# A planned mLSTM and MoE kernel: wider first tiles, GpSimd as a second home for weight pieces, and a plan that reckons with TensorE's clock

## The chip, the cores and the metric

The kernel runs on one core of one Trainium2 chip. The core's engines are TensorE (PE in the profile; PEld is its weight loading), VectorE (DVE), ScalarE (ACT), GpSimd (POOL) and SyncE (SP), which issues the DMAs. Each works through its own queue in order, and semaphores tie the queues together. The metric is device microseconds (us) of one execution.

## The reference, cut to what matters

Four sequences of 768 steps with 8 heads of width 40 go through an mLSTM (a gated linear attention), and its 3072 x 320 result through two feed-forward blocks (called MoE here) of width 2048. All of it is float32.

```python
for t in range(S):                       # per batch and head
    m_new = max(f[t] + m, i[t])
    C = exp(f[t] + m - m_new) * C + exp(i[t] - m_new) * outer(v[t], k[t])
    n = exp(f[t] + m - m_new) * n + exp(i[t] - m_new) * k[t]
    y[t] = sigmoid(o[t]) * (C @ q[t]) / max(abs(n @ q[t]), 1.0)
x = y                                    # 3072 x 320
h = x @ w_in;  x = max(0.01 * h, h) @ w_out
h = max(x @ w_in2, 0);  out = (h * h) @ w_out2
```

## The kernel before, in words

The sequence is cut into 6 chunks of 128 steps. A chunk holds 4 batches, so it makes a block of 512 tokens. `attention(c)` does the mLSTM of a chunk in parallel form, in 8 groups of 4 heads (two groups a batch). On TensorE a group is a decay row spread over 128 partitions (L615, chunk 0 only), the scores (L635), the state's part (L645) and the values (L651, or L656 to L661 in bfloat16 thirds). Between them stand an exp on ScalarE (L626), a mask on GpSimd (L629) and a product on VectorE (L638). The two groups of a batch end in `hs` (L682 or L684), then in a denominator `d` (L736 to L738), the gated `y` (L740, L743), three transposes (L750) and the split of x into a high part `xH` (L755) and a low part `xL` (L756).

The MoE computes float32 products out of float32r ones, by high and low parts. `weight(layer, j)` loads one of 16 slices of a layer's weights, puts the high part into `w` (L401) and the low parts beside it: L405 (512 and 64 columns) and the "stack" L410 (64 x 128), all on VectorE. `moe_h` multiplies x by a slice (8 matmuls, L434) into `hp`, of which there are 2 buffers. ScalarE and VectorE make `gH` and `gL` of it (L440 to L442), and `out1` adds 8 matmuls (L465 to L467, L470, L471) into three accumulators. One slice on one block is 16 matmuls of up to 512 columns. Layer 0 and then layer 1 run over the 6 blocks, with the attention of later chunks in between.

Block 0 of layer 0 is done in two halves of 256 columns, since batches 0 and 1 are ready before 2 and 3. The second half runs `lag` = 7 slices behind the first (L765 to L772).

No engine's order is written by hand. `op(...)` records a node with an engine, an estimated duration and its buffers. `Sched.forward` (L137) plays these nodes with the estimates, `backward` (L113) turns the result into latest start times, and after six passes the best plan is issued. The keys of the first pass come from the table `ORDER`. When TensorE has nothing ready in the plan, a `warm` product may be put in: an empty matmul that only keeps TensorE at work, into `hp` (L322) or, adding zero, into an accumulator (L478). A node with `alt` may go to GpSimd instead of VectorE.

Of the kernel before, what the change touches and what calls it, by code (L numbers as in the profile page):

```python
# [30 lines left out]
ORDER = dict(pe0=7000, ld2=80, kv=-2.33, ks=6.4, g2=32.54, z=-15.1, lag=7, m0=0.71, o0=1.85, a04=-6.78, a0s=4.65, a1=29.4, a1s=5.72, a1ld=23.83, w0=-33.49, ws=2.64, bias=1.13, c0=-19.03, cs=13.0, cld=31.54, wl=1.51, outk=2.04)  # L31
SHARE = 0.6
PASSES = 6
# [13 lines left out]
class Node:  # L47
    __slots__ = ("eng", "dur", "fn", "key", "deps", "outs", "ndep", "ready", "allocs", "bufs", "end", "start", "table", "lat", "seq", "alt", "after", "first", "bank")


class Sched:
# [10 lines left out]
    def op(self, eng, dur, key, fn, r=(), w=(), table=None, lat=0, alt=None, after=0):  # L62
# [4 lines left out]
        n.eng, n.dur, n.fn, n.key, n.table, n.lat = eng, dur, fn, key, table, lat  # L67
# [69 lines left out]
    def forward(self):  # L137
# [24 lines left out]
        out, now, dma_free, done, last = [], 0.0, 0.0, 0, 0.0  # L162
        while done < len(self.nodes):

            for e, cand in ready.items():
# [3 lines left out]
                for n in sorted(cand, key=lambda n: (n.key, n.seq)):  # L169
                    if all(b.live or (b.first is n and queue[b.tag][-1] is b and free[b.tag] > 0) for b in n.bufs):  # L170
                        pick = n
                        break
                if pick is None:
                    if e == "PE" and self.idle and (now < 12000 or now - last > 300) and (fill := next((f for f in self.idle if f[1].live and f[2].start is None), None)):
                        n = Node()
                        n.eng, n.dur, n.fn, n.allocs, n.seq, n.start, n.key = e, 430 if now < 6800 else 215, fill[0], [], -1, now, 0
                        n.bufs, n.deps = [], []
                        out.append(n)
                        busy[e] = n
                        heapq.heappush(at, (now + n.dur, 0, -1))  # L180
                    continue
# [38 lines left out]
            if seq < 0:  # L220
                busy["PE"] = None
                last = now - 200
                continue
            n = self.nodes[seq]
            if what == 0:
                busy[n.eng] = None
                last = now if n.eng == "PE" else last
# [35 lines left out]
def mlstm_moe_kernel(  # L263
# [111 lines left out]
    def weight(layer, j, key):  # L375
# [49 lines left out]
    def moe_h(layer, c, lo, n, j, key, xk):  # L425
# [10 lines left out]
        op("PE", 8 * mm(n), key, pe, r=[(w, "H"), (w, "L"), (w, "C")] + [(x, k) for k in xk for x in (xH, xL)], w=[(hp, 0)])  # L436
# [14 lines left out]
    def out1(c, lo, n, j, key):  # L451
# [20 lines left out]

        rd = [(w, "H"), (w, "L"), (w, "Lc"), (gH, 0), (gL, 0)]
        op("PE", 3 * mm(n), key, lambda: ab(0, 256, 1024), r=rd, w=[(a[0], lo)])
        op("PE", 3 * mm(n), key, lambda: ab(1, 384, 1152), r=rd, w=[(a[1], lo)])
        x = op("PE", 2 * mm(n), key, cc, r=rd + ([(warm, 0)] if c == 0 and j == NF - 1 and lo == 0 else []), w=[(a[2], lo)])
        if j == NF - 1 and n < BLK and lo == 0:
            sc.idle.append((lambda: T.matmul(a[2].t, warm.t, zeros(), start=False, stop=False), a[2], x))  # L478
        if last:
            x2[c] = x = sb(f"x2_{c}", [128, 3, BLK])  # L480
            key -= 100
            rd = [[(a[t], l) for l in range(0, BLK, n)] for t in range(3)]
# [18 lines left out]
    def out2(c, j, key):  # L501
# [5 lines left out]
        for b in range(B):  # L507
# [9 lines left out]
            op("PE", 3 * mm(DM), key, pe, r=[(w, "H"), (w, "L"), (gH, 0), (gL, 0)], w=[(a, 0)])  # L517
# [11 lines left out]
    def attention(c, keys, ld):  # L529
# [23 lines left out]
        op("PE", 380, k0, gate_T, r=[(G_sb, f"A{p}"), (G_sb, f"c{p}"), (G_sb, f"w{p}"), (ident, 0)], w=[(gp, 0)])  # L553
# [305 lines left out]
```

## Time and profile before

| | |
|---|---|
| time, median of 3 runs | 857.66 us (857.45 to 859.22) |
| the profiled execution's own time | 857.15 us |
| its span, first to last instruction | 855.1 us |
| mean granted clock of TensorE | 0.988 |
| busy: TensorE, VectorE, ScalarE, GpSimd | 842.0, 541.4, 464.9, 77.8 us |

A row of a timeline gives the start, the time taken, the engine with the source line, the operands, and in brackets how long the engine was idle before and what ended that. Consecutive matmuls overlap in the records, so the time from start to start is what one costs. A matmul of float32 operands stands as two records. The clock is a share of full speed: 1.00 is 2.4 GHz and 0.50 is 1.2 GHz.

### The profile page before, as it was taken

The page shows a single profiled execution, that of the slowest core. Times are in us where ns is not written, and L with a number is a line of the kernel's source. Part 1 is how long each engine was busy: PE and PEld are TensorE (multiplying, and loading weights), DVE is VectorE, ACT ScalarE, POOL GpSimd, SP SyncE. Part 2 cuts the span into 40 slices and gives each one's busy share as a digit, 9 for nine tenths or more (in the row PEclk, how much of TensorE's full clock was granted, in tenths as well). Part 3 has the DMA queues.
Part 4 walks back from the last instruction along what each step waited for, and adds up shares of the span by engine and source line. Part 5 has one row for each costly group of instructions (what it writes and reads, how often), then busy time and mean ns, then how long its engine had stood idle before and what let it go on. Part 6 is the DMA issues. An engine that isn't in the chain of part 4 may idle for free.

```text
span 855.1 us, 14028 instructions
## 1 busy us (share of the span) xinstructions
PE 842.0 (98%) x5310; PEld 729.9 (85%) x5310; DVE 541.4 (63%) x1008; ACT 464.9 (54%) x946; POOL 77.8 (9%) x101
## 2 busy tenths in 40 slices
PE   9899999999999999999999999999999999999998
PEld 7689999788778788788888889999999999999997
DVE  7799876767676776667576899453443443533433
ACT  6577638656765776577455675343333433433332
POOL 2231204103010311011000000000000000000000
PEclk8899999999999999999999999999999999999999
DMA  8675325435343543453232442000000000000000
GB/s 226 222 233 183 118 73 181 140 111 172 103 137 114 165 138 109 152 166 118 77 103 72 165 136 69 1 31 1 1 32 1 14 17 1 31 1 1 32 1 31
DMA packets 52211, 78.60 MB, mean 92 GB/s; under 512 B 4336, under 2 KB 40784, under 8 KB 52144
## 3 DMA queue, kind: packets, MB, share of 16 engines
q1 hardware_dynamic: 52144, 77.71, 28.8%
q8 instruction: 42, 0.69, 0.3%
q14 instruction: 25, 0.20, 0.1%
HBM read 54.26 MB, written 4.01 MB: 68 GB/s over the span
## 4 chain that ended last, share of the span: by engine, by line
PE 82%; DVE 6%; ACT 4%; SPq 3%; DMA 3%; issue 1%; ACTq 0%; DVEq 0%
PE hp L434 36%; PE acc L465 4%; PE acc L467 4%; PE acc L466 4%; SPq L581 3%; PE acc L515 3%; PE acc L514 3%; PE acc L513 3%; PE attS L635 3%; PE acc L470 2%; PE atty L645 2%; PE acc L471 2%; PE atty L651 2%; DMA T<-X 2%; PE atty L515 1%
## 5 line engine op out<-in xcount | busy, mean ns | idle before, releaser
L434 PE MATMUL hp<-xH,w 128*128 128x512 f32 (+1 forms) x1040 | 294.8, 381 | 0.3 <-DVE gL L442 0.3
L434 PEld LDWEIGHTS hp<-xH,w 128*128 128x128 f32 x1040 | 183.5, 189 | 29.2 <-DVE gL L442 0.9
L434 PE MATMUL hp<-xL,w 128*128 128x512 f32 (+1 forms) x624 | 199.1, 375 | 0.0
L446 DVE TENSOR_TENSOR g<-g 128x512 f32<-128x512 f32 x96 | 66.3, 691 | 118.4 <-ACT g L445 118.3
L434 PEld LDWEIGHTS hp<-xL,w 128*128 128x128 f32 x624 | 115.9, 189 | 22.4
L445 ACT ACTIVATE g<-hp 128x512 f32<-128x512 f32 x96 | 57.3, 597 | 129.4 <-PE hp L434 129.4
L448 DVE TENSOR_TENSOR gL<-g,gH 128x512 fp32r<-128x512 f32 x96 | 66.4, 692 | 56.4 <-ACT gH L447 56.4
L447 ACT CAST gH<-g 128x512 fp32r<-128x512 f32 x96 | 59.6, 620 | 70.4 <-DVE g L446 70.4
L442 DVE TENSOR_TENSOR gL<-hp,gH 128x512 fp32r<-128x512 f32 (+1 forms) x112 | 68.3, 610 | 34.7 <-ACT hp L441 34.2
L465 PE MATMUL acc<-gH,w 128*128 128x512 f32 (+1 forms) x224 | 86.1, 384 | 0.0
L440 ACT ACTIVATE gH<-hp 128x512 fp32r<-128x512 f32 (+1 forms) x112 | 59.6, 532 | 48.4 <-PE hp L434 39.3
L467 PE MATMUL acc<-gL,w 128*128 128x512 f32 (+1 forms) x224 | 81.3, 363 | 0.0
L466 PE MATMUL acc<-gH,w 128*128 128x512 f32 (+1 forms) x224 | 81.0, 362 | 0.0
L515 PE MATMUL acc<-w,gL 128*128 128x320 f32 x192 | 59.3, 309 | 0.0
L514 PE MATMUL acc<-w,gH 128*128 128x320 f32 x192 | 59.3, 309 | 0.0
L513 PE MATMUL acc<-w,gH 128*128 128x320 f32 x192 | 59.2, 308 | 0.0
L441 ACT ACTIVATE hp<-hp 128x512 f32<-128x512 f32 (+1 forms) x112 | 59.1, 528 | 0.0
L626 ACT ACTIVATE aw<-aw,cs 128x128 f32<-128x128 f32 x160 | 50.8, 391 | 12.2 <-DMA aw<-Adram 12.1
L629 POOL TENSOR_SCALAR_AFFINE_SELECT aw<-aw 128x512 f32<-128x512 f32 x48 | 33.5, 697 | 196.5 <-ACT aw L626 174.0
L467 PEld LDWEIGHTS acc<-gL,w 128*128 128x128 f32 x224 | 42.6, 190 | 6.9 <-DVE gL L442 0.2
L465 PEld LDWEIGHTS acc<-gH,w 128*128 128x128 f32 x224 | 42.7, 191 | 5.3
L466 PEld LDWEIGHTS acc<-gH,w 128*128 128x128 f32 x224 | 42.8, 191 | 4.9
(163 smaller groups left out, 1515.1 us busy)
## 6 DMA issues: line engine op xcount, KB each, us to landing
T<-X SPq DMA_DIRECT2D x144, 120.0 KB
x<-in_wts_dram SPq DMA_DIRECT2D x16, 704.0 KB
aw<-Adram SPq DMA_DIRECT2D x40, 256.0 KB
nat<-in_nat_dram SPq DMA_DIRECT2D x24, 328.0 KB
qkr<-in_qk_dram SPq DMA_DIRECT2D x16, 360.0 KB
X<-in_wts_dram SPq DMA_DIRECT2D x8, 704.0 KB
T<-in_wts_dram SPq DMA_DIRECT2D x8, 704.0 KB
og<-in_og_dram SPq DMA_DIRECT2D x12, 320.0 KB
```

The source lines that it names most:

```text
L434: T.matmul(hp.t[:, 0:n], w.t[:, col:col + 128], x.t[:, kt, o], start=(s == 0), stop=(s == 7))
L440: op("ACT", act(n, True), key, lambda: A.activation(gH.t[:, 0:n], h(), AF.Prelu, alpha=0.01), r=[(hp, 0)], w=[(gH, 0)])
L442: op("DVE", dve(n), key, lambda: V.tensor_tensor(out=gL.t[:, 0:n], in0=h(), in1=gH.t[:, 0:n].bitcast(F32), op=ALU.subtract), r=[(hp, 0), ( ...
L446: op("DVE", dve(n), key, lambda: V.tensor_tensor(out=g.t, in0=g.t, in1=g.t, op=ALU.mult), r=[(g, 0)], w=[(g, 0)])
L447: op("ACT", act(n), key, lambda: A.copy(gH.t, g.t), r=[(g, 0)], w=[(gH, 0)])
L448: op("DVE", dve(n), key, lambda: V.tensor_tensor(out=gL.t, in0=g.t, in1=gH.t.bitcast(F32), op=ALU.subtract), r=[(g, 0), (gH, 0)], w=[(gL, 0)])
L465: T.matmul(a[t].t[:, o], w.t[:, hc:hc + 128], gH.t[:, 0:n], start=first, stop=False)
L466: T.matmul(a[t].t[:, o], w.t[:, lc:lc + 128], gH.t[:, 0:n], start=False, stop=False)
L467: T.matmul(a[t].t[:, o], w.t[:, hc:hc + 128], gL.t[:, 0:n], start=False, stop=last)
L513: T.matmul(a.t[:, 0:DM], gH.t[:, s], wH, start=first, stop=False)
L514: T.matmul(a.t[:, 0:DM], gH.t[:, s], wL, start=False, stop=False)
L515: T.matmul(a.t[:, 0:DM], gL.t[:, s], wH, start=False, stop=last)
```

## The change

- Block 0 in wider tiles: slices 0 to 6 are still done in halves. From slice 7 on (L797 to L804 of the changed kernel) one tile of 512 columns serves both halves, and the second half of slices 0 to 6 runs between these tiles. Nine slices go from 2 x 256 to 512 columns.
- The stack (L441, before L410) and low parts of at most 512 columns (L436, before L405) get `alt`, so the plan may give them to GpSimd. In the built program 14 of the 16 stacks, all 16 pieces of 64 columns and one of 512 columns of layer 0 are there, and 2 stacks of layer 1.
- The plan now models TensorE's clock: each TensorE node has a `load`, and where the plan finds too little of it, later nodes take twice their duration. An empty product is put in only where nothing is ready and the recent load is low. The old rule asked for an early time, or for 300 ns without work. Short attention pieces are marked `small`, are kept together, and a change to a long piece costs 85 ns in the plan.
- `ORDER` has new numbers. The plan before has 18 empty products into `hp` and 15 of L478, the changed one 15 and none.

```diff
-ORDER = dict(pe0=7000, ld2=80, kv=-2.33, ks=6.4, g2=32.54, z=-15.1, lag=7, m0=0.71, ...
+ORDER = dict(pe0=6853.31, ld2=74.38, kv=1.55, ks=6.4, g2=29.83, z=-14.43, lag=7, m0=0.89, ...
+WINDOW = 3413
+BUSY = 0.38
+KEEP = 0.43
+STAY = 3000
...
+        def clock():
+            return 1 if stream.get(int(now // WINDOW) - 1, 0) >= BUSY * WINDOW else 2
...
+        def idles():
+            while hist and hist[0][1] < now - WINDOW:
+                hist.pop(0)
+            return sum(r * (e - max(b, now - WINDOW)) for b, e, r in hist) < KEEP * WINDOW
...
-                        pick = n
-                        break
+                        if pick is None:
+                            pick = n
+                        elif n.small:
+                            pick = n
+                        if e != "PE" or pick.small or not small or n.key > pick.key + STAY:
+                            break
+                if e == "PE" and pick is None and idles() and (fill := next((f for f in self.idle if f[1].live and f[2].start is None), None)):
...
-                    if e == "PE" and self.idle and (now < 12000 or now - last > 300) and (fill := ...
...
+                if e == "PE":
+                    dur += 85 if small and not n.small else 0
+                    small = n.small
+                    dur *= clock()
+                    streams(n.load, dur)
...
-        op("DVE", dve(128), key, lambda: stack(V), r=[(fb, fr), (w, "C")], w=[(w, "C")])
+        op("DVE", dve(128), key, lambda: stack(V), r=[(fb, fr), (w, "C")], w=[(w, "C")], alt=("POOL", pool(128), lambda: stack(G)))
...
-            op("DVE", dve(n), key, lambda: low(V, o, n, s0), r=[(fb, fr), (w, "H")], w=w_)
+            op("DVE", dve(n), key, lambda: low(V, o, n, s0), r=[(fb, fr), (w, "H")], w=w_, **(dict(alt=("POOL", pool(n), lambda: low(G, o, n, s0))) if n <= 512 else {}))
...
-    LAG = ORDER["lag"]
-    for i in range(NF + LAG):
-        for s in range(2):
-            j = i - LAG * s
-            if 0 <= j < NF:
+    LAG = min(ORDER["lag"], NF // 2 - 1)
+    for i in range(max(NF, 2 * LAG)):
+        for s, j in ((0, i), (1, i - LAG)):
+            n = 256 if j < LAG else BLK
+            if 0 <= j < (LAG if s else NF):
                 key = ORDER["m0"] * U * i + s
-                moe_h(0, 0, 256 * s, 256, j, key, (2 * s, 2 * s + 1))
-                out1(0, 256 * s, 256, j, key + ORDER["o0"] * U)
+                moe_h(0, 0, 256 * s, n, j, key, (2 * s, 2 * s + 1) if n < BLK else range(4))
+                out1(0, 256 * s, n, j, key + ORDER["o0"] * U)
```

TensorE ahead of the first MoE matmul, before: L478 with `warm` is an empty product, L750 the transposes of `y`, L615 a decay row, L434 the first MoE matmul.

```order
L478 LDWEIGHTS warm
L478 MATMUL acc_239<-warm 128x512
L478 LDWEIGHTS warm
L478 MATMUL acc_239<-warm 128x512
L750 MATMUL attm<-ident,y 128x128 x3
L478 LDWEIGHTS warm
L478 MATMUL acc_239<-warm 128x512
L478 LDWEIGHTS warm
L478 MATMUL acc_239<-warm 128x512
L615 MATMUL attS<-G_sb,ident 128x128 x4
L434 MATMUL hp<-xH,w_334 128x256 x4
L434 MATMUL hp<-xL,w_334 128x256 x2
```

The same place in the changed order (L683 are the values of batch 1, L782 the transposes, L647 decay rows, L740 the update, L667 scores, L492 the zeroing of an accumulator, L465 the first MoE matmul):

```order
L683 MATMUL atty<-nat,aw 128x42 x4
L782 MATMUL attm<-ident,y 128x128 x3
L647 MATMUL attS<-G_sb,ident 128x128 x4
L740 MATMUL attm<-wv,nat 40x42 x16
L667 MATMUL attS<-w_132 128x128 x4
L782 MATMUL attm<-ident,y 128x128 x3
L492 LDWEIGHTS warm
L492 MATMUL acc_390<-warm 128x512
L647 MATMUL attS<-G_sb,ident 128x128 x4
L465 MATMUL hp<-xH,w_360 128x256 x4
L465 MATMUL hp<-xL,w_360 128x256 x2
```

The empty products are gone, and a score piece and its decay row have moved ahead of the second transposes.

GpSimd before, from the fifth mask on: L629 masks, L740 the gating of `y`, L696 a product with the gates.

```order
L629 AFFINE_SELECT aw<-aw 128x512 x2
L740 TENSOR_TENSOR og<-og,d 128x320
L629 AFFINE_SELECT aw<-aw 128x512
L696 TENSOR_TENSOR wv<-nat,ex 128x336 x2
L629 AFFINE_SELECT aw<-aw 128x512
L740 TENSOR_TENSOR og<-og,d 128x320
L629 AFFINE_SELECT aw<-aw 128x512 x3
```

The same place in the changed order (L661 masks, L772 the gating, L728 the product; L441 stacks and L436 low parts of weight slices, `w_360` being slice 0 and `w_476` slice 3):

```order
L661 AFFINE_SELECT aw<-aw 128x512 x2
L772 TENSOR_TENSOR og<-og,d 128x320
L661 AFFINE_SELECT aw<-aw 128x512
L441 TENSOR_TENSOR w_360<-x_2_270,w_360 64x128
L436 TENSOR_TENSOR w_360<-x_2_270,w_360 128x64
L441 TENSOR_TENSOR w_400<-x_3_362,w_400 64x128
L436 TENSOR_TENSOR w_400<-x_3_362,w_400 128x64
L728 TENSOR_TENSOR wv<-nat,ex 128x336
L661 AFFINE_SELECT aw<-aw 128x512
L728 TENSOR_TENSOR wv<-nat,ex 128x336
L441 TENSOR_TENSOR w_462<-x_2_270,w_462 64x128
L436 TENSOR_TENSOR w_462<-x_2_270,w_462 128x64
```

Between the same masks and products now stand two pieces of each weight slice. The mask behind `w_400` has four of them ahead of it.

TensorE at slice 7 of block 0, before (`w_779` is slice 7 and `w_334` slice 0): a half tile of slice 7, then the second half of slice 0.

```order
L434 MATMUL hp<-xH,w_779 128x256 x4
L434 MATMUL hp<-xL,w_779 128x256 x2
L434 MATMUL hp<-xH,w_779 128x256
L434 MATMUL hp<-xL,w_779 128x256
L434 MATMUL hp<-xH,w_334 128x256 x4
L434 MATMUL hp<-xL,w_334 128x256 x2
L434 MATMUL hp<-xH,w_334 128x256
L434 MATMUL hp<-xL,w_334 128x256
```

The same place in the changed order (`w_757` is slice 7, `w_360` slice 0): slice 7 with 512 columns, then the second half of slice 0.

```order
L465 MATMUL hp<-xH,w_757 128x512 x4
L465 MATMUL hp<-xL,w_757 128x512 x2
L465 MATMUL hp<-xH,w_757 128x512
L465 MATMUL hp<-xL,w_757 128x512
L465 MATMUL hp<-xH,w_360 128x256 x4
L465 MATMUL hp<-xL,w_360 128x256 x2
L465 MATMUL hp<-xH,w_360 128x256
L465 MATMUL hp<-xL,w_360 128x256
```

The half tile of slice 7 has become one of full width; the second half of slice 0 still follows it with 256 columns.

## Rows read from the trace of the kernel before

**Rows 1.** The page, engines: busy us, share, instructions.

```profile
PE 842.0 (98%) x5310; PEld 729.9 (85%) x5310; DVE 541.4 (63%) x1008; ACT 464.9 (54%) x946; POOL 77.8 (9%) x101
```

**Rows 2.** Busy time by stretch: length, PE, PEld, DVE, ACT, POOL, clock, DMA share, GB/s.

```profile
16.00:29.00 13.00, 13.00 (x54) 10.52 (x53) 8.92 (x20) 7.06 (x20) 1.53 (x2) 0.50 0.84 245
36.00:57.00 21.00, 20.62 (x183) 18.34 (x183) 20.51 (x40) 17.79 (x50) 7.46 (x7) 1.00 0.59 190
57.00:60.00 3.00, 3.00 (x16) 3.00 (x16) 3.00 (x7) 2.58 (x7) 2.07 (x3) 0.51 0.94 333
84.00:87.00 3.00, 3.00 (x17) 2.95 (x16) 2.56 (x5) 1.28 (x4) 1.15 (x2) 0.56 0.29 65
120.00:360.00 240.00, 234.09 (x1721) 195.55 (x1720) 170.31 (x349) 160.63 (x356) 42.99 (x55) 1.00 0.44 136
```

**Rows 3.** TensorE's waits by releaser: us in total, times, longest.

```profile
PE atty L645 <- DVE hs L686: 2.7, 4, 0.8
PE atty L659 <- DVE x L665: 1.9, 3, 1.3
```

**Rows 4.** Timeline of TensorE, 25 to 63 us: start, us, instruction, idle before.

```profile
25.53 1.93 PE L651 MATMUL atty<-nat,aw 128*128 128x42 f32 x8
35.39 0.72 PE L434 MATMUL hp<-xH,w 128*128 128x256 f32 x4
51.02 0.81 PE L478 MATMUL acc<-warm 128*128 128x512 bf16 x3
61.89 0.38 PE L478 MATMUL acc<-warm 128*128 128x512 bf16 x1
62.57 0.74 PE L434 MATMUL hp<-xH,w 128*128 128x256 f32 x4 [0.30 <-DVE gL L442]
```

**Rows 5.** Timeline of VectorE, 20 to 36 us.

```profile
20.13 0.68 DVE L638 TENSOR_TENSOR aw<-aw,acc 128x512 f32<-128x512 f32 x1
27.83 0.17 DVE L736 SCALAR_TENSOR_TENSOR d<-hs 128x8 f32<-128x8 f32 x1 [3.67 <-ACT hs L682]
30.99 1.21 DVE L405 TENSOR_TENSOR w<-x,w 128x512 fp32r<-128x512 f32 x1
34.34 0.55 DVE L756 TENSOR_TENSOR xL<-attm,xH 128x384 fp32r<-128x384 f32 x1
34.81 0.68 DVE L405 TENSOR_TENSOR w<-x,w 128x512 fp32r<-128x512 f32 x1
```

**Rows 6.** Timeline of TensorE, 57 to 69 us and 499 to 503 us.

```profile
57.30 0.41 PE L465 MATMUL acc<-gH,w 128*128 128x256 f32 x1
59.00 1.05 PE L434 MATMUL hp<-xH,w 128*128 128x256 f32 x4
66.64 0.74 PE L434 MATMUL hp<-xH,w 128*128 128x256 f32 x4
67.70 0.64 PE L434 MATMUL hp<-xH,w 128*128 128x256 f32 x4
68.65 0.28 PE L465 MATMUL acc<-gH,w 128*128 128x256 f32 x1
...
499.04 1.07 PE L434 MATMUL hp<-xH,w 128*128 128x512 f32 x4
502.67 1.07 PE L434 MATMUL hp<-xH,w 128*128 128x512 f32 x4
```

**Rows 7.** VectorE's groups by form, L410 and L405: count, busy us, mean ns, idle.

```profile
L410 DVE TENSOR_TENSOR w<-x,w 64x128 fp32r<-64x128 f32 x16 | 5.1, 317 | 0.5
L405 DVE TENSOR_TENSOR w<-x,w 128x64 fp32r<-128x64 f32 x16 | 4.5, 288 | 0.1
```

**Rows 8.** Timeline of GpSimd, 0 to 32 us.

```profile
1.07 0.29 POOL masks.py:199 TENSOR_SCALAR_AFFINE_SELECT ident<-ident 128x128 f32<-128x128 f32 x1
30.34 1.31 POOL L740 TENSOR_TENSOR og<-og,d 128x320 f32<-128x320 f32 x1 [7.58 <-PE attm L708]
```

More of the change, by code (lines that the diff above doesn't have):

```diff
@@ L47 @@
 class Node:
-    __slots__ = ("eng", "dur", "fn", "key", "deps", "outs", "ndep", "ready", "allocs", "bufs", "end", "start", "table", "lat", "seq", "alt", "after", "first", "bank")
+    __slots__ = ("eng", "dur", "fn", "key", "deps", "outs", "ndep", "ready", "allocs", "bufs", "end", "start", "table", "lat", "seq", "alt", "after", "first", "bank", "small", "load")
 class Sched:
@@ L161, in forward, with streams @@
                 heapq.heappush(at, (n.after, 1, n.seq))
-        out, now, dma_free, done, last = [], 0.0, 0.0, 0, 0.0
+        out, now, dma_free, done, small = [], 0.0, 0.0, 0, False
+        stream, hist = {}, []
+        def clock():
+            return 1 if stream.get(int(now // WINDOW) - 1, 0) >= BUSY * WINDOW else 2
+        def streams(load, dur):
+            t, r = now, load / dur
+            while t < now + dur:
+                k = int(t // WINDOW)
+                u = min(now + dur, (k + 1) * WINDOW)
+                stream[k] = stream.get(k, 0) + r * (u - t)
+                t = max(u, t + 1e-3)
+            hist.append((now, now + dur, r))
+        def idles():
+            while hist and hist[0][1] < now - WINDOW:
+                hist.pop(0)
+            return sum(r * (e - max(b, now - WINDOW)) for b, e, r in hist) < KEEP * WINDOW
         while done < len(self.nodes):
@@ L170, in forward @@
                     if all(b.live or (b.first is n and queue[b.tag][-1] is b and free[b.tag] > 0) for b in n.bufs):
-                        pick = n
-                        break
-                if pick is None:
[L174 to L180, printed above, removed]
+                        if pick is None:
[5 more added lines that the diff above has]
+                if e == "PE" and pick is None and idles() and (fill := next((f for f in self.idle if f[1].live and f[2].start is None), None)):
+                    n = Node()
+                    n.eng, n.dur, n.fn, n.allocs, n.seq, n.start, n.key = e, 215 * clock(), fill[0], [], -1, now, 0
+                    n.bufs, n.deps = [], []
+                    streams(213, n.dur)
+                    out.append(n)
+                    busy[e] = n
+                    heapq.heappush(at, (now + n.dur, 0, -1))
+                    continue
+                if pick is None:
                     continue
@@ L221, in forward @@
                 busy["PE"] = None
-                last = now - 200
                 continue
@@ L226, in forward @@
                 busy[n.eng] = None
-                last = now if n.eng == "PE" else last
             elif what == 1:
@@ L471, in cc @@
             T.matmul(a[2].t[:, o], w.t[:, 640:768], gL.t[:, 0:n], start=False, stop=last)
+        reg = lambda t: [(a[t], l) for l in range(lo, lo + n, 256)]
         rd = [(w, "H"), (w, "L"), (w, "Lc"), (gH, 0), (gL, 0)]
[L474 to L477, printed above, removed]
+        op("PE", 3 * mm(n), key, lambda: ab(0, 256, 1024), load=3 * n / 2.4, r=rd, w=reg(0))
+        op("PE", 3 * mm(n), key, lambda: ab(1, 384, 1152), load=3 * n / 2.4, r=rd, w=reg(1))
+        x = op("PE", 2 * mm(n), key, cc, load=2 * n / 2.4, r=rd + ([(warm, 0)] if c == 0 and j == NF - 1 and lo == 0 else []), w=reg(2))
+        if j == NF - 1 and lo == 0 and c == 0:
             sc.idle.append((lambda: T.matmul(a[2].t, warm.t, zeros(), start=False, stop=False), a[2], x))
@@ L481, in out1 @@
             key -= 100
-            rd = [[(a[t], l) for l in range(0, BLK, n)] for t in range(3)]
+            rd = [[(a[t], l) for l in range(0, BLK, 256)] for t in range(3)]
             op("ACT", act(BLK, True), key, lambda: A.copy(x.t[:, 0], a[0].t), r=rd[0], w=[(x, 0)])
```

28 lines of the change are left out of this document (14 added, 14 removed).

## The prediction, made blind

> **What bounds the kernel now.** I read the page first: TensorE is busy for 842.0 us of the 855.1 us span [rows 1]. VectorE, the next, has 63%. So the time is TensorE's work plus what TensorE loses, and a change is worth what it takes from either. Next I read the busy times by stretch. TensorE is busy for 20.62 us of the 21 us from 36 to 57 us, and for 234.09 of 240 us from 120 to 360 us [rows 2]. VectorE is as full as TensorE from 36 to 57 us (20.51 us) but not later. The clock column shows the second kind of loss, which busy time hides: 0.50 from 16 to 29 us, 0.51 from 57 to 60 and 0.56 from 84 to 87 [rows 2]. Last I read the waits: the largest are attention pieces waiting for VectorE, 2.7 us at L645 and 1.9 us at L659 [rows 3]. They lie behind 140 us, where the change edits nothing but the plan.
>
> **Term 1, wider tiles.** Eight matmuls of 256 columns take 68.65 - 67.70 = 0.95 us. A half tile has sixteen, so a slice in two halves costs 4 x 0.95 = 3.80 us. A slice in one tile of 512 columns costs 502.67 - 499.04 = 3.63 us [rows 6]. Nine slices change: 9 x 0.17 = 1.5 us, and all of it is on TensorE. ScalarE and VectorE get nine tiles fewer to evict; I count that at nothing, as TensorE waited for an eviction only 0.30 us at 62.57 [rows 4].
>
> **Term 2, kept together.** The first four matmuls of a slice take 0.74 us behind an attention piece and 0.64 us behind a MoE piece [rows 6]. So a change from one to the other costs 0.10 us. Counted in the orders, these changes fall from 119 to 110: 0.9 us.
>
> **Term 3, until the first MoE matmul at 35.39 [rows 4].** The chain there runs through the last values of batch 1 (25.53), their denominator on VectorE (27.83, after 3.67 us idle), and `xL` of batch 1 (34.34) [rows 4, 5]. TensorE was full all the way to these values, half of it at the low clock [rows 2]. The changed order has one zeroing and one empty product less ahead of them, 0.4 us each at that clock, and two opening products less, some 0.2 us each: they start some 1.3 us earlier, at 24.2, and the denominator at 26.5. But VectorE then has more queued ahead of `xL`: the gate parts that stood before the idle stretch, the start of slice 2, the product of one more group. By the durations in the timeline these are 8.5 us against 34.34 - 27.83 = 6.5. So `xL` starts at 35.0, 0.7 us late. In return a score piece and a decay row (about 1 us each) are done by then, and one of them stood behind the first slices before. I take 0 for the term. From below: if the clock stays up, the values wait only for the product of their weights, which ends at 20.13 + 0.68 = 20.8 [rows 5], 4.7 us before 25.53; less the 2.0 us of longer queue this is a gain of 2.7. From above: 2.0 lost, if that queue hides nothing.
>
> **Term 4, no empty products before the MoE.** Before, they filled the waits around 30 us, and the clock was back when the MoE began. Now TensorE runs the same pieces without them and may begin the MoE at 1.2 GHz. Eight matmuls of 256 columns then cost 59.00 - 57.30 = 1.70 us against 0.95 [rows 6]. I take one such group, 0.8 us lost; from 0 to three groups, 2.3.
>
> **Term 5, gaps inside block 0.** Empty products and waits there: 0.81 us at 51.02, 0.38 at 61.89 with 0.30 behind it [rows 4], about 1.5 in all. An empty product also keeps back what becomes ready while it runs. I take half, 0.7 gained; bounds 1.5 gained and 1.0 lost.
>
> **Term 6, the clock inside block 0.** The stretches at 57 and 84 cost 3 x 0.49 and 3 x 0.44 = 2.8 us of full-speed work [rows 2], while TensorE was full. The changed order puts nothing empty there and has denser tiles, which should spare one of the two: 1.4 gained; bounds 2.8 gained and 2.8 lost, as no row shows the changed order's clock.
>
> **Term 7, GpSimd.** VectorE gives up 14 stacks at 0.317 us and 16 pieces at 0.288 [rows 7], and one of 512 columns (0.68 [rows 5]): 9.7 us. GpSimd's nearest row in size is 0.29 us for 128 columns with one operand, the largest 1.31 us for 320 with two [rows 8]; I take 0.4 and 0.3, some 11 us on an engine that is mostly idle there (7.46 of 21 us [rows 2]). While the 1.31 us operation ran, the 512-column subtraction on VectorE took 1.21 us instead of 0.68 [rows 5, 8]: 0.53 lost in 1.31. At that rate 11 us on GpSimd take back 4.4 of the 9.7. What is left, 5 us, lies beside a full TensorE, so I count 0; bounds 1.0 gained and 1.5 lost.
>
> The Trainium skill speaks against this edit: "SBUF — State Buffer", section "Who interferes with whom", has a VectorE operation with two inputs in SBUF and a GpSimd operation that reads SBUF exclude each other for a whole instruction, and the second one waits. The trace agrees in kind, as the longer subtraction shows, but not in full: it lost less than half of the other's time. By the rule VectorE could lose all of GpSimd's time, which is the third rival below.
>
> **Term 8, the rest.** Waits behind 120 us: 240 - 234.09 = 5.9 us up to 360 [rows 2]. The largest are waits for VectorE [rows 3]; the new plan moves them, and I see no reason for more or fewer. 0, with 2 either way.
>
> **The sum.** -1.5 - 0.9 + 0 + 0.8 - 0.7 - 1.4 + 0 + 0 = -3.7 us, against the profiled execution's own 857.15 us (0.5 under the median of the runs): 853.4 us.
>
> **The rivals.**
> - *The clock stays up at the start.* The changed order brings scores and a decay row forward from 10 to 16 us, which may hold the clock at 2.4 GHz. Then the MoE starts 2.7 us earlier and at full clock: 853.4 - 2.7 - 0.8 = 849.9. Against it: the pieces are the same few-row scores and values that ran when it fell before.
> - *The start eats it.* Without empty products the gaps stay gaps, `xL` is late by the full 2.0, term 5 gives 0 and term 6 gives 0: 853.4 + 2.0 + 0.7 + 1.4 = 857.5, no change. For it: the old empty products stand exactly in these gaps. Against it: they ran where TensorE had nothing to do anyway. This is also the case in which the plan's clock is not the chip's, so that the change does not do what it says.
> - *VectorE loses as much as GpSimd takes.* If VectorE stands still for all of the 11 us, it is 11 - 9.7 = 1.3 us fuller than before where it is as full as TensorE, from 36 to 57 us [rows 2], and the MoE's first slices come that much later: 853.4 + 1.3 = 854.7. For it: the subtraction that grew from 0.68 to 1.21 us [rows 5]. Against it: that one lost 0.53 of 1.31 us. (This is the rule of "SBUF — State Buffer" as the Trainium skill has it.)
> - *A stack on GpSimd becomes the wait.* The last two of the eight matmuls of `moe_h` read the stack, and TensorE is in order: behind a late stack everything waits, attention too. On GpSimd a stack stands behind masks that wait for an exp on ScalarE, and behind operations of up to 1.31 us [rows 8]. With half of the excess over its 0.317 us on VectorE hidden, 14 slices wait 0.5 us each: 7.0 us, 860.4. It decides from 3.7 / 14 = 0.26 us a slice on. Against it: GpSimd is idle for two thirds of the time from 36 to 57 us [rows 2].
>
> **How the numbers follow.** Forecast 0.37, clock up 0.15, start eats it 0.26, fuller VectorE 0.09, late stacks 0.13. The forecast's own range by terms 3 to 8 is 850.5 to 856. What this kernel's measurement can tell from no change is 0.2%, 1.7 us: below 855.9 is faster, above 859.4 slower. Of the forecast 0.35 lies below 855.9, of the fuller VectorE 0.08, of the clock staying up all 0.15, and a fifth of the second rival, 0.05: 0.63. Above 859.4 lie the late stacks and a fifth of the second rival: 0.18. The rest, 0.19, is no change. The range from 848.8 to 859.6 leaves out the late stacks and the tail of the first rival.
>
> **What would show it.** Term 1: 16 matmuls of 512 columns in 3.63 us from slice 7 on. Term 3: the first MoE matmul between 34.5 and 36 us, and the denominator of batch 1 near 26.5. Term 4: a clock near 0.5 just before and a little after it. Term 6: at most one low stretch between 40 and 120 us. Term 7: VectorE's busy time 3 to 8 us lower up to 120 us, and no row in which TensorE waits for L441 on GpSimd. Terms 5 and 8: TensorE's waits up to 400 us within 2 us of before. The prediction is wrong if the first MoE matmul comes at 33 us or at 38, if L441 stands among TensorE's releasers with over 3 us, or if the clock falls three times or more behind 40 us.

## The result, and the profile after

The changed kernel takes 866.67 us (median of 4, 865.37 to 868.61) against 857.56 us of the kernel before on the same chip. The ratio is 1.0116, with a 95% interval of 1.0087 to 1.0145. The forecast was 853.4, with a range to 859.6: wrong in sign, and outside the range. The ratios and intervals of this document leave out one run as a slow one, an execution of b_noempty at 871.52 us. The profiled execution of the changed kernel took 865.59 us with a span of 863.8, and its mean granted clock is 0.972, where before has 0.988.

The page's engines, against [rows 1]: TensorE is busy for 6.9 us more with 164 records fewer.

```profile
PE 848.9 (98%) x5146; PEld 730.2 (85%) x5148; DVE 531.8 (62%) x968; ACT 463.4 (54%) x928; POOL 102.7 (12%) x132
```

Busy time by stretch of the changed kernel, columns as in [rows 2]; the clock is the third number from the right.

```profile
16.00:29.00 13.00, 12.78 (x66) 11.51 (x67) 9.54 (x25) 7.25 (x20) 1.49 (x3) 0.55 0.60 160
29.00:36.00 7.00, 4.94 (x47) 4.23 (x46) 6.92 (x12) 3.73 (x12) 3.35 (x4) 0.50 0.87 286
36.00:48.00 12.00, 12.00 (x56) 11.69 (x56) 11.18 (x18) 8.03 (x17) 7.66 (x10) 0.50 0.49 175
48.00:57.00 9.00, 9.00 (x99) 8.43 (x99) 7.81 (x13) 6.71 (x20) 2.13 (x5) 1.00 0.80 256
57.00:60.00 3.00, 3.00 (x26) 2.75 (x25) 3.00 (x9) 3.00 (x10) 2.28 (x4) 1.00 0.67 152
60.00:84.00 24.00, 23.39 (x163) 21.25 (x161) 22.00 (x41) 18.61 (x41) 10.41 (x15) 0.93 0.64 211
84.00:87.00 3.00, 3.00 (x46) 2.82 (x46) 2.80 (x6) 2.16 (x7) 1.82 (x3) 0.76 1.00 394
87.00:120.00 33.00, 32.64 (x227) 28.88 (x227) 27.83 (x55) 17.21 (x40) 13.79 (x17) 0.91 0.32 98
120.00:360.00 240.00, 233.91 (x1612) 191.42 (x1612) 164.88 (x340) 157.89 (x342) 41.55 (x51) 0.99 0.42 133
```

Read the rows from 29 to 48 us first. Before, the clock was back at full when the MoE began ([rows 2], 36 to 57 us: 1.00). Now it stays at 1.2 GHz until 48 us, and from 36 to 48 TensorE is busy for 12.00 of 12 us with 56 matmul records; from 48 to 57 it has 99 in 9 us. The busy share of 100% does not show this. Behind 57 us the clock falls four more times, at 68.5, 85.5, 95.8 and 119.7 us, which the shares of 0.93, 0.76, 0.91 and 0.99 hold.

TensorE's waits by releaser, against [rows 3]:

```profile
PE atty L677 <- DVE hs L718: 3.8, 5, 1.3
PE attS L667 <- DVE aw L670: 1.7, 4, 1.0
PE attm L782 <- ACT C L749: 1.1, 1, 1.1
PE atty L691 <- DVE x L697: 0.5, 3, 0.2
```

The timeline of TensorE in the changed kernel, against [rows 4, 6]:

```profile
24.55 1.93 PE L683 MATMUL atty<-nat,aw 128*128 128x42 f32 x8
26.27 0.88 PE L782 MATMUL attm<-ident,y 128*128 128x128 f32 x3
26.95 1.91 PE L647 MATMUL attS<-G_sb,ident 96*128 96x128 f32 x8
28.79 1.35 PE L740 MATMUL attm<-wv,nat 128*40 128x42 f32 x32
30.15 2.07 PE L667 MATMUL attS<-w 40*128 40x128 f32 x8
35.17 2.07 PE L647 MATMUL attS<-G_sb,ident 96*128 96x128 f32 x8 [0.97 <-DVE aw L670]
36.90 1.20 PE L465 MATMUL hp<-xH,w 128*128 128x256 f32 x4
38.75 1.77 PE L683 MATMUL atty<-nat,aw 128*128 128x42 f32 x8
...
63.47 0.49 PE L782 MATMUL attm<-ident,y 128*128 128x128 f32 x3
63.80 0.98 PE L683 MATMUL atty<-nat,aw 128*128 128x42 f32 x8
64.71 1.16 PE L667 MATMUL attS<-X 40*128 40x128 f32 x8
66.47 1.06 PE L677 MATMUL atty<-C,X 40*128 40x42 f32 x8 [0.61 <-DVE hs L718]
67.46 0.39 PE L496 MATMUL acc<-gH,w 128*128 128x256 f32 x1
68.52 1.91 PE L465 MATMUL hp<-xH,w 128*128 128x512 f32 x4
```

The eight products of the first MoE group run from 36.90 to 38.75, 1.85 us, where the same group costs 0.95 at full clock [rows 6]. Ahead of them stand the pieces of attention alone: values, transposes, decay row, update, scores. At 63.47 the same kinds run for 4.0 us in a row; 0.61 us of them a wait; eight matmuls later the clock falls, and four of 512 columns take 1.91 us instead of 1.07 [rows 6]. That the one causes the other is not shown by these rows (see a_all and a_break).

To set the parts against the sum, I took the time from the start of each matmul to the start of the next and compared it with the median for the same shape at full clock in the trace before. That median is "work". An empty product counts in full; of the others, what exceeds the median is put to the low clock where the granted clock was 0.50, to waits where TensorE stood over 60 ns, and else to "other" (changes between kinds are there). The clock goes first, so the two waits of 1.08 and 0.97 us just ahead of the first MoE matmul stand in the changed kernel's 23.4. A few matmul records are missing from each trace, and their time falls to a neighbour. Each execution's span is the sum plus 4.6 us; the last four columns are runs of the next section:

| us of the profiled execution | before | changed | a_empty | a_front | b_front | b_front_gps |
|---|---|---|---|---|---|---|
| work | 810.0 | 808.6 | 808.6 | 808.6 | 810.0 | 810.0 |
| empty products | 15.4 | 6.9 | 10.9 | 14.3 | 15.6 | 14.2 |
| waits | 8.2 | 11.9 | 14.0 | 12.1 | 9.0 | 10.3 |
| low clock | 7.4 | 23.4 | 18.8 | 9.5 | 1.5 | 0.0 |
| other | 9.5 | 8.4 | 7.5 | 9.3 | 9.2 | 9.7 |

Of the changed kernel's 16.0 us more at the low clock, 5.6 lie between 16 and 36 us, 5.7 between 36 and 57, and 4.7 between 57 and 127. It saves 8.4 us of empty products and 1.4 of work, and waits 3.7 longer. With the two waits counted as waits, some 14 us of the 16 are left to the clock and the waits grow by nearly 6.

### The profile page after: what moved, and what is told of

Read it like the earlier page. It is cut to its first block, busy times and chain, and to the rows that moved or that the text cites. A ratio compares the mean times of both kernels' runs of the same rounds, so it can differ in the third digit from the quotient of the medians.

```text
span 863.8 us, 13656 instructions
## 1 busy us (share of the span) xinstructions
PE 848.9 (98%) x5146; PEld 730.2 (85%) x5148; DVE 531.8 (62%) x968; ACT 463.4 (54%) x928; POOL 102.7 (12%) x132
## 4 chain that ended last, share of the span: by engine, by line
PE 70%; DVE 11%; SPq 5%; ACT 5%; DMA 4%; issue 3%; POOL 1%; ACTq 0%; DVEq 0%; POOLq 0%
PE hp L465 31%; SPq L613 5%; PE acc L547 3%; PE acc L546 3%; PE acc L545 3%; PE acc L496 3%; PE acc L498 3%; PE acc L497 3%; PE attS L667 2%; PE atty L683 2%; DMA aw<-Adram 2%; PE acc L501 1%; PE atty L677 1%; DMA T<-X 1%; PE acc L502 1%
## 5 line engine op out<-in xcount | busy, mean ns | idle before, releaser
L465 PE MATMUL hp<-xH,w 128*128 128x512 f32 (+1 forms) x995 | 292.3, 392 | 0.9 <-DVE gL L473 0.8
L465 PEld LDWEIGHTS hp<-xH,w 128*128 128x128 f32 x995 | 181.5, 192 | 32.3 <-DVE gL L473 1.6
L465 PE MATMUL hp<-xL,w 128*128 128x512 f32 (+1 forms) x597 | 197.8, 386 | 0.0
L465 PEld LDWEIGHTS hp<-xL,w 128*128 128x128 f32 x597 | 112.8, 191 | 23.6
L478 ACT CAST gH<-g 128x512 fp32r<-128x512 f32 x96 | 59.5, 620 | 65.8 <-DVE g L477 65.8
L496 PE MATMUL acc<-gH,w 128*128 128x512 f32 (+1 forms) x206 | 84.5, 410 | 0.0
L497 PE MATMUL acc<-gH,w 128*128 128x512 f32 (+1 forms) x206 | 79.2, 384 | 0.0
L661 POOL TENSOR_SCALAR_AFFINE_SELECT aw<-aw 128x512 f32<-128x512 f32 x48 | 37.6, 784 | 186.6 <-ACT aw L658 173.5
L658 ACT ACTIVATE aw<-aw,cs 128x128 f32<-128x128 f32 x160 | 50.9, 392 | 11.2 <-DMA aw<-Adram 10.3
L498 PEld LDWEIGHTS acc<-gL,w 128*128 128x128 f32 x206 | 40.0, 194 | 11.0 <-DVE gL L473 3.4
L496 PEld LDWEIGHTS acc<-gH,w 128*128 128x128 f32 x206 | 40.1, 195 | 5.5
L497 PEld LDWEIGHTS acc<-gH,w 128*128 128x128 f32 x206 | 40.1, 195 | 5.4
```

Of the source, the lines that this page charges most:

```text
L465: T.matmul(hp.t[:, 0:n], w.t[:, col:col + 128], x.t[:, kt, o], start=(s == 0), stop=(s == 7))
L478: op("ACT", act(n), key, lambda: A.copy(gH.t, g.t), r=[(g, 0)], w=[(gH, 0)])
L496: T.matmul(a[t].t[:, o], w.t[:, hc:hc + 128], gH.t[:, 0:n], start=first, stop=False)
L497: T.matmul(a[t].t[:, o], w.t[:, lc:lc + 128], gH.t[:, 0:n], start=False, stop=False)
L498: T.matmul(a[t].t[:, o], w.t[:, hc:hc + 128], gL.t[:, 0:n], start=False, stop=last)
```

## The experiments

All ran beside the kernel before, whose median was between 855.5 and 857.0 us there. Names with b_ start from the kernel before in its own order, unless a new plan is mentioned; names with a_ start from the changed kernel. Clocks are means over a kernel's executions. A profile is one execution, and the kernel before alone has mean clocks from 0.986 to 0.998, so the mean over executions says more than where the clock falls in one profile.

**b_noempty and a_empty: the empty products alone.**

```diff
# b_noempty: the kernel before without its 15 empty products of L478
+            if n.seq < 0 and n.fn is sc.idle[1][0]:
+                continue
# a_empty: the changed order with 15 put in by hand (node: count)
+    EMPTY = {68: 1, 113: 3, 100: 3, 132: 2, 464: 2, 162: 3, 175: 1}
+            for _ in range(EMPTY.get(n.seq, 0)):
+                sc.idle[1][0]()
```

> The kernel before with its plan and order untouched, but the 15 empty products of L478 not issued. If their absence is what cost the changed kernel its time (theory E), the clock stays at 1.2 GHz from 16 us until well behind 40 us instead of 29.7 us, and the time rises from 857.6 to 862 to 866 us. If the GpSimd pieces (theory G) or the new order itself (theory P) are the cause, the time stays within 2 us of 857.6.

> The changed kernel with its plan and order untouched, and 15 empty products issued at the places that they had before (before and behind the transposes of batches 0 and 1, before the first MoE results, at the gates of chunk 1). Theory E: the clock is back by 34 us instead of 48 us and the time falls from 866.7 to 859 to 862 us; falls of the clock behind 60 us stay as they are. Theories G and P: the time stays at 866 to 868 us, since TensorE is full there and empty products only delay it.

b_noempty: 859.05 us over nine executions, 1.0026 (0.9995 to 1.0057), clock 0.982 where before had 0.992 beside it. a_empty: 863.09 us, 1.0085 (1.0052 to 1.0117), clock 0.982 where the changed kernel had 0.970. So the products hold part of the clock in both orders. In time that is some 3 us by the medians each way (859.05 against 856.2, and 863.09 against 866.67), and neither is clear of noise: the first interval takes in 1, the second overlaps that of the changed kernel. Both missed the times that theory E expected, and more than half of the loss stays, so the missing products are not the whole cause. a_empty's profile agrees: the clock is back by 30 us instead of 48, but falls again behind 40 us.

```profile
29.00:36.00 7.00, 5.49 (x60) 4.05 (x60) 6.90 (x11) 3.50 (x11) 2.82 (x4) 0.93 0.78 263
36.00:48.00 12.00, 10.94 (x67) 10.42 (x67) 11.94 (x19) 8.11 (x19) 8.04 (x10) 0.72 0.51 183
```

**a_pieces_dve and b_gps: GpSimd alone.**

```diff
# a_pieces_dve: the changed plan's order, the pieces issued on VectorE
-alt=("POOL", pool(128), lambda: stack(G))
+alt=("POOL", pool(128), lambda: stack(V))
# (the same for low(G, o, n, s0))
# b_gps: the order before, stacks and 64-column pieces issued on GpSimd
-lambda: stack(V)
+lambda: stack(G)
-lambda: low(V, o, n, s0)
+lambda: low(G if n <= 64 else V, o, n, s0)
```

> The changed kernel with its plan, and each stack and low part that the plan gave to GpSimd issued on VectorE instead, at the same place of the plan. Theory G: the time falls from 866.7 to 861 or less, and the clock falls less often. Theory E: 865 to 869 us, the clock low until 45 us or later; VectorE's busy time rises by 5 to 9 us up to 120 us.

> The kernel before, in its own order, with the 16 stacks and the 16 subtractions of 64 columns of the first half of block 0 issued on GpSimd instead of VectorE. Theory: term 7, about nothing (856 to 859), since these pieces are not waited for at the end of the chain. Rival: GpSimd's pieces, longer than VectorE's, become waits of TensorE in 35 to 57 us, and the time is 860 to 866, above all if a wait there takes the clock down again.

a_pieces_dve: 868.62 us, 1.0145 (1.0109 to 1.0181), no faster than the changed kernel (1.0087 to 1.0145): GpSimd is not what costs. b_gps (whose edit also moves the 16 stacks of layer 1): 855.53 us, 0.9999 (0.9976 to 1.0022). Term 7 holds: nothing, as long as the clock is what it was.

**b_wide: the wide tiles alone, with the planner and the table of before.** The plan is made anew, since the nodes are others.

```diff
-    LAG = ORDER["lag"]
-    for i in range(NF + LAG):
+    LAG = min(ORDER["lag"], NF // 2 - 1)
+    for i in range(max(NF, 2 * LAG)):
# (the loop's body, and the accumulator regions of out1, as in the changed kernel)
```

> The kernel before, its planner and its table of numbers, with block 0 in tiles of 512 columns from slice 7 on and nothing else of the change. By the sum of the prediction 1.5 us less of TensorE's work: 856.1 us, 855 to 857.5. If the wide tiles are the cause of the loss (theory W), 862 us or more, with the clock low more often from 60 to 120 us than in the kernel before.

864.27 us, 1.0085 (1.0048 to 1.0122), and the clock is that of before (0.991). In its profiled execution the work is 1.4 us less, as term 1 has it, but the waits are 19.0 us instead of 8.2. Its waits by releaser:

```profile
PE hp L434 <- ACT xH L756: 3.3, 4, 0.9
PE attm L751 <- DVE y L744: 3.1, 4, 1.3
PE hp L434 <- DVE gL L442: 3.0, 7, 1.1
```

Before, a MoE group waited for VectorE once, for 0.30 us [rows 4]. The waits cost more than the edit saves. Tiles and plan change together here, so the run doesn't show which of the two makes these waits; the clock, as theory W had it, does not.

**a_noclock, a_nogroup, a_halves, a_oldtable, a_plain: the planner's rules one by one.** Each makes a new plan.

```diff
# a_noclock: the plan's clock always full, the empty products by the rule of before
-            return 1 if stream.get(int(now // WINDOW) - 1, 0) >= BUSY * WINDOW else 2
+            return 1
-                if e == "PE" and pick is None and idles() and (fill := ...
+                if e == "PE" and pick is None and self.idle and (now < 12000 or now - last > 300) and (fill := ...
# a_nogroup: small pieces not kept together, no 85 ns
-                        elif n.small:
-                            pick = n
...
-                    dur += 85 if small and not n.small else 0
# a_halves: block 0 in halves throughout; a_oldtable: ORDER of before
# a_plain: a_noclock and a_nogroup together
```

> The changed kernel whose plan takes TensorE's clock as always full and sets the empty products by the rule of before (35 of them); wide tiles, GpSimd pieces, grouping and the new table of numbers stay. Theory 'the clock model is what costs': the plan no longer puts matmuls at doubled times, the empty products stand where the work thins out, the mean granted clock comes back to .99 and the time to 850 to 855 us (the changed kernel's base of about 847 us plus some three quarters of 8 us lost to the clock). Rival 'the grouping, the wide tiles or the new table is what lets the clock fall': the clock stays near .973 to .982 and the time at 861 to 868.

> The changed kernel whose plan does not group the small pieces and does not price a change between kinds at 85 ns; clock model, wide tiles and GpSimd pieces stay. Theory 'the clock model is what costs': the time stays within 3 us of the changed kernel's, 863 to 869, with the clock at .970 to .980. Rival 'runs of small pieces are what lets the clock fall behind 60 us': the half-clock stretches behind 60 us go, the clock rises to .985 or more, and the time is 855 to 860.

> The changed kernel with the first block of the MoE in halves of 256 columns throughout, as before; everything else as changed. If the wide tiles bring what term 1 of the prediction says, the base rises by 1.5 us and, with the clock unchanged near .973, the time is 866 to 870. Rival 'the wide tiles empty the list of work that TensorE draws on around 36 to 57 us and so hold the clock down': the clock rises to .985 and the time is 855 to 861.

> The changed kernel with the table of numbers of before. If the refit of the table costs: clock .980 or more and 858 to 864. If it is the rules (clock model and few empty products): clock .965 to .975 and 866 to 874, the refit being worth nothing or a few us in the changed kernel's favour.

> a_noclock without the grouping of small pieces: planner's rules as before, with wide tiles, GpSimd pieces and the new table. If grouping is what keeps the clock of the new plans below that of the old ones with the same count of empty products: clock .990 and 857 to 862 (the idle time of a new order, as with b_wide, stays). Rival 'the new table or the GpSimd pieces do it': clock .984 as in a_noclock, time 863 to 868.

| | us | ratio, 95% | clock |
|---|---|---|---|
| a_noclock | 865.40 | 1.0105 (1.0063 to 1.0146) | 0.984 |
| a_nogroup | 867.96 | 1.0128 (1.0082 to 1.0173) | 0.976 |
| a_halves | 875.95 | 1.0223 (1.0186 to 1.0260) | 0.965 |
| a_oldtable | 870.26 | 1.0139 (1.0103 to 1.0176) | 0.974 |
| a_plain | 865.78 | 1.0113 (1.0075 to 1.0150) | 0.984 |

The theory that the plan's model of the clock is the cause fell by half. Without it the clock comes back to 0.984 (10.7 us at the low clock in its profile instead of 23.4), but the 35 empty products cost 8.4 us more and the waits 2.7, and the time is that of the changed kernel. Grouping and the new table don't explain it either: without them the time is the same or worse. In halves throughout, the changed planner is 9 us worse still, past both expectations; this speaks against the wide tiles as the cause, but its plan is another one too. The seven kernels with a plan made anew so far, the changed one among them, stand at 864 us or above; what all seven share is that they are not the order of before.

**b_front and b_all: more empty products in the order of before.** If stretches of small matmuls are what lets the clock fall, products of 512 columns among them should hold it where before falls too.

```diff
+    EARLY, LATE = {81: 1, 51: 1, 76: 1, 84: 1, 59: 1, 105: 1}, {86: 1, 100: 1, 116: 1}
+            for _ in range(EARLY.get(n.seq, 0)):
+                sc.idle[0][0]()
+            for _ in range(LATE.get(n.seq, 0)):
+                sc.idle[1][0]()
# b_all: LATE has also {172: 1, 174: 1, 210: 1, 212: 1, 544: 1}
```

> The kernel before in its own order, with 9 more empty products of 512 columns put between its small matmuls where before shows 12 to 30 us. Theory 'what lets the clock fall are stretches of small matmuls, however busy TensorE is': the half-clock stretch of 16 to 30 us shrinks or goes, the mean clock rises from .990 to .995 or more, and the time falls from 856 to 851 to 854. Rival 'the fall at 16 us has another cause than what TensorE is given': the stretch stays, the 9 products cost .2 to .43 us each, 2 to 4 us, and the time is 858 to 860.

> As b_front, with 5 more empty products where before shows 54 to 57 and 81 to 85 us. By the theory the later half-clock stretches go in most executions too: clock .995 to .998, five times .21 us of cost against 1 to 3 us of clock, so the same as b_front or up to 2 us less, 850 to 854. By the rival 859 to 861, the clock unchanged at .990.

b_front: 852.50 us, 0.9960 (0.9940 to 0.9980), clock 0.998. b_all: 852.50 us, 0.9942 (0.9921 to 0.9963), clock 0.999. Both beat the kernel before; the five further products of b_all change nothing that can be told from b_front. The timeline of b_front on TensorE, and then its stretches:

```profile
11.49 0.38 PE L322 MATMUL hp<-warm 128*128 128x512 bf16 x1
11.71 1.05 PE L615 MATMUL hp<-G_sb,ident 96*128 96x128 f32 x8
12.60 0.38 PE L322 MATMUL hp<-warm 128*128 128x512 bf16 x1
17.41 0.98 PE L651 MATMUL atty<-nat,aw 128*128 128x42 f32 x8
30.99 0.72 PE L434 MATMUL hp<-xH,w 128*128 128x256 f32 x4
```

```profile
16.00:29.00 13.00, 11.12 (x104) 8.15 (x102) 12.79 (x28) 8.46 (x24) 3.29 (x3) 1.00 0.87 254
48.00:57.00 9.00, 9.00 (x89) 8.81 (x89) 8.88 (x18) 8.39 (x26) 3.98 (x5) 0.81 0.84 287
84.00:87.00 3.00, 3.00 (x27) 2.90 (x26) 2.91 (x11) 2.97 (x8) 0.00 (x0) 1.00 0.71 253
```

An empty product costs 0.22 us there (11.49 to 11.71). From 16 to 29 us the clock is 1.00 instead of 0.50 [rows 2], TensorE does 104 records instead of 54, and the first MoE matmul starts at 30.99 instead of 35.39 [rows 4]. VectorE is now the full engine (12.79 of 13 us) ahead of the MoE. One fall is left, between 48 and 57 us (0.81). From 84 to 87 us the clock is 1.00 where it was 0.56, though all nine products stand ahead of the MoE; what spares this stretch is not shown.

**a_front and a_all: the same in the changed order.** 25 and 38 more empty products, between 12 and 56 us and, in a_all, up to 105 us.

```diff
# a_front
+    EARLY = {81: 1, 76: 1, 51: 1, 84: 1, 105: 1, 59: 1, 78: 1}
+    LATE = {108: 1, 86: 1, 68: 1, 113: 2, 89: 1, 116: 1, 100: 3, 132: 2, 464: 1, 110: 1, 118: 1, 162: 2, 175: 1}
# a_all: 13 nodes more in LATE, one each
```

> The changed kernel in its own order, with 25 more empty products of 512 columns where its trace shows 12 to 56 us. If the clock is the whole cause: the half-clock stretch of 17 to 48 us goes, clock .990 or more, and with the gains of the wide tiles and the GpSimd pieces the time is 848 to 853. Rival 'its order has losses of its own': clock .990 and 854 to 859. If the products don't hold the clock: .975 and 866 or more.

> As a_front, with 13 more empty products where the changed kernel's trace shows 56 to 105 us (13 times .21 us, 2.8 us). If the later stretches at the lower clock (68 to 72, 86 to 89, 96 to 99, 120 to 126 us) are all that is left: clock .997, 849 to 853, 0 to 3 us less than a_front. Rival: clock .997 in both and this one 2 to 3 us slower.

a_front: 861.35 us, 1.0053 (1.0032 to 1.0074), clock 0.987. a_all: 864.71 us, 1.0112 (1.0076 to 1.0147), clock 0.985. Both are slower than any time expected with the clock held. a_front's stretches:

```profile
16.00:29.00 13.00, 12.38 (x114) 9.80 (x115) 11.77 (x29) 7.89 (x23) 3.04 (x4) 1.00 0.69 203
29.00:36.00 7.00, 4.96 (x21) 4.15 (x21) 7.00 (x11) 4.92 (x13) 3.18 (x5) 0.58 0.89 305
36.00:48.00 12.00, 11.16 (x84) 10.14 (x83) 11.94 (x20) 8.25 (x21) 6.63 (x8) 0.96 0.53 185
60.00:84.00 24.00, 23.95 (x179) 21.57 (x179) 21.93 (x44) 18.48 (x37) 8.25 (x13) 0.87 0.67 224
87.00:120.00 33.00, 32.64 (x226) 29.23 (x225) 27.25 (x52) 15.70 (x38) 15.34 (x20) 0.88 0.23 70
```

The long stretch at 1.2 GHz is gone up to 29 us and from 37 to 64, and 5 us of time with it. What stays lies behind 57 us (0.87 and 0.88 where b_front has 1.00), and the first MoE matmul comes at 34.64 us, 3.7 later than in b_front. So the clock at the start is one cause, worth 5.3 us, and the new order has losses of its own. By the table above a_front loses 8.0 us more to the clock than b_front, and 3.1 more to waits.

a_all tries the same on what stays, and it gains nothing: 13 more products among the matmuls behind 56 us cost 3 us and don't raise the mean clock. In its profile three of them run at 61.5, 62.9 and 73.2 us, and the clock falls at 64.1 and 74.4 all the same. So a few such products, which hold the clock ahead of the MoE in b_front, did not hold it there.

**a_break: are long runs of small matmuls what takes the clock down behind 57 us?** Between 57 and 126 us, the longest run on TensorE without a product of 256 or 512 columns is 2.1 us in the traces of before, b_front and b_wide. It is 4.7, 4.0 and 2.6 us in the changed kernel's, and 5.0, 3.5 and 2.6 in a_front's. Such runs are not needed for a fall, though: before falls at 84.4 us without one.

```diff
# on a_plain, behind 30 us: after 1.6 us of small pieces, a long piece goes first
+                        elif not n.small:
+                            pick = n
+                        if e != "PE" or not pick.small or row < 1600 or now < 30000:
+                            break
```

> a_plain (wide tiles, GpSimd pieces, the new table, the planner's rules of before) whose plan, behind 30 us, prefers a product of the MoE to a small piece once small pieces have run for some 2 us on TensorE. If the long runs of small matmuls take the clock down: the falls between 57 and 126 us (three stretches of 3.4 or 6.8 us in a_plain) mostly go, the mean clock rises from .984 to .990 or more and the time from 865.8 to 859 to 862 (the idle time stays). If something else of the new order does it: clock .984, 864 to 868.

868.56 us, 1.0148 (1.0107 to 1.0189), clock 0.983. The longest runs became 3.0 and 2.3 us, from 3.6 and 2.4, and one of a_plain's two falls there is gone (57 to 64 us; the one near 100 came at 112). But the fall at 17 us, which a_plain's profile doesn't have, came back in the new plan. Clock and time are those of the rival (0.984, 864 to 868) but for 0.6 us. As the new plan brought its own falls, this is inconclusive: that long runs of small matmuls precede some of the falls is seen in the traces; that they cause those behind 57 us is not shown.

**b_front_gps: b_front with GpSimd's pieces.** The edits of b_front and b_gps together.

> b_front with the 16 stacks and 16 subtractions of 64 columns issued on GpSimd. If VectorE's work ahead of 57 us is on the path once the clock is held: 1 to 2 us less than b_front, 850.5 to 851.5. If term 7 (nothing) holds: 852 to 853.

850.56 us, 0.9932 (0.9908 to 0.9956), clock 0.999: the fastest of all, 6 us under before. In its profile the clock never falls ahead of the last 2 us:

```profile
16.00:29.00 13.00, 10.65 (x100) 8.17 (x101) 12.73 (x28) 8.98 (x25) 3.37 (x4) 1.00 0.87 249
36.00:48.00 12.00, 11.59 (x89) 10.22 (x89) 11.34 (x20) 9.75 (x25) 6.57 (x9) 1.00 0.62 216
60.00:84.00 24.00, 24.00 (x219) 22.84 (x219) 21.48 (x44) 17.32 (x38) 10.23 (x14) 1.00 0.59 193
```

The 1.9 us between the medians of b_front and b_front_gps were not timed beside each other, and the intervals of the two ratios overlap. They are no more than a sign that VectorE's relief is worth something once VectorE is the full engine.

## Why the prediction was wrong

The step that failed is the price of the clock, terms 4 and 6: 0.8 lost and 1.4 gained, with bounds of a few us. Measured, the low clock costs 16.0 us more than before (some 14 without the two waits inside it), while the missing empty products give back 8.4 and the wider tiles 1.4. The reasoning went wrong at one place: "I take one such group, 0.8 us lost". Term 4 priced the low clock per MoE group, up to three of them, and took for granted that MoE products bring the clock back at once. In the trace the clock stayed at 1.2 GHz for 11 us of mixed MoE and attention pieces behind the first of them (36.90 to 48.0), and had been there since 17.3. The empty products that the change removes stood ahead of this stretch and were read as fillers of waits, of which the time is worth nothing. That products there hold the clock is shown clear of noise by a_front and b_front, where more of them are worth 3 to 5 us. That the 15 removed ones alone did so is seen in the mean clocks of a_empty and b_noempty; their 3 us each way are not clear of noise.

- Term 1, wider tiles: right. The work is 1.4 us less, forecast 1.5.
- Term 2, fewer changes between kinds: not shown. "Other" is 1.1 us less, forecast 0.9, but it runs from 7.5 to 9.3 in the three executions of the changed order above, and the term was not tried alone.
- Term 3, the first MoE matmul: 36.90 instead of 34.5 to 36, 1.5 us late; the forecast was 0. The denominator came near the time it gave (26.85 against 26.5), and `xL` at 35.85 against 35.0. VectorE's rows:

```profile
26.85 0.17 DVE L768 SCALAR_TENSOR_TENSOR d<-hs 128x8 f32<-128x8 f32 x1
32.22 0.94 DVE L436 TENSOR_TENSOR w<-x,w 128x512 fp32r<-128x512 f32 x1
35.85 0.54 DVE L788 TENSOR_TENSOR xL<-attm,xH 128x384 fp32r<-128x384 f32 x1
```

  On TensorE the decay row still stands ahead of the first MoE matmul. It waited for VectorE until 35.17 and took 1.73 us at the low clock, not the 1 us of full clock, so it ended at 36.90, behind `xL` (36.39).
- Term 5, gaps inside block 0: empty products between 36 and 127 us fell from 1.8 us to none, but waits there rose from 0.4 to 1.3: 1.0 gained, forecast 0.7.
- Term 6 said "should spare one of the two" stretches. Neither was spared: four came in their place. Denser tiles are not what it takes: b_front's clock is 1.00 from 84 to 87 us in tiles of 256 columns. The term's 2.8 us was also short, as its rows of 3 us cut the stretches off: in the trace before they run from 57.0 to 60.5 and from 84.4 to 87.8 us, 3.4 us of full-speed work.
- Term 7, GpSimd: the sum (0) agrees with b_gps, and VectorE is 4.5 us less busy from 7 to 120 us, inside the 3 to 8 given. The durations were far off. GpSimd's rows by form:

```profile
L441 POOL TENSOR_TENSOR w<-x,w 64x128 fp32r<-64x128 f32 x14 | 9.5, 676 | 23.2 <-ACT w L432 21.8 <-POOL aw L661 1.3
L436 POOL TENSOR_TENSOR w<-x,w 128x64 fp32r<-128x64 f32 x16 | 8.6, 537 | 0.9
L436 POOL TENSOR_TENSOR w<-x,w 128x512 fp32r<-128x512 f32 x1 | 1.5, 1513 | 0.1
```

  0.676 and 0.537 us where I took 0.4 and 0.3: 19.6 us on GpSimd, not 11. On VectorE the 512-column subtraction went from 751 to 790 ns, 15 x 0.039 = 0.6 us: but that is one row, and the total says it better. The 48 pieces that b_gps moves took 14.2 us on VectorE before (5.1, 4.6 and 4.5) and take 36.9 on GpSimd (11.8, 16.1 and 9.0), and VectorE is 8.9 us less busy (532.5 against 541.4): it loses 5.3 us, about a seventh of what GpSimd takes, and the rival in which it loses all of it falls. The rule of "SBUF — State Buffer" in the Trainium skill, section "Who interferes with whom", is not refuted by that: it has the second of the two wait, which can be GpSimd, and GpSimd's pieces did take longer than forecast. The term's "0.53 lost in 1.31" was misread, too: the subtraction began at 30.99, and only the last 0.66 us of GpSimd's operation (30.34 to 31.65) lay beside it, so it lost most of that overlap and not less than half.
- Term 8, waits behind 120 us: 2.9 us more behind 127 us, where I saw no reason for any. b_wide shows how large this can be: 11 us more of waits with wide tiles and a plan made anew.
- Rivals: no row has TensorE wait for L441, so the late stacks didn't come. "The start eats it" came nearest, with a third of the price: 4.1 us over the forecast, measured 13.3. Its reason (the plan's clock is not the chip's) fits the falls, but a_noclock, which drops that model, is no faster. "The clock stays up at the start" is what b_front does: the MoE starts 4.4 us earlier, against the 2.7 forecast.

What stays open: why the new orders lose more to the clock than the old one behind 57 us, and which of the planner's rules, if any, sets their waits. a_all and a_break didn't settle the first; for the second, the waits by the same reckoning are 14 to 19 us in the profiles of a_noclock, a_nogroup, a_halves, a_oldtable and a_plain, and so never below the changed kernel's 11.9.

## What to carry to other kernels

Read the granted clock beside the busy share, and price a stretch at the low clock by all the work that will run in it, not by the first group: here 31 us on end ran at half speed. Before an empty product is counted as a filler, look at what the clock does behind it; a few more ahead of the MoE, at 0.22 us each, were the cheapest gain of this study (0.4 to 0.6%), while a_all's behind 56 us gained nothing. And where a planner orders everything, an edit that makes it plan anew can move the time by more than the edit is worth (all seven new plans here were slower), so try the edit in the old order first.

## What was not expected of the hardware

- One and the same kernel varies with its clock. Over the 74 executions of the kernel before beside the experiments, the time runs from 851.2 us (clock 0.998) to 859.7 (0.988), and a line through them gives 0.63 us of time for each us lost to the clock (one minus the mean clock, times the time; correlation 0.79).
- TensorE can be busy without a gap and stay at 1.2 GHz: from 36 to 48 us of the changed kernel, 12.00 of 12 us, clock 0.50.
- GpSimd's subtraction of 64 x 128 elements takes 0.45 to 0.98 us (median 0.63) against 0.30 on VectorE; the 2 stacks of layer 1 took 1.30 and 1.79 there.
